# Layer 1's second mixer product: six of eight pairs of token tiles by Strassen's algorithm

## The chip, the cores and the metric

The kernel runs on one core of one Trainium2 chip. The time is device microseconds of one execution, from its launch to its end; 2512.71 us is the median of three runs (2511.84 to 2514.52). The profile is one further execution, read by engine: PE is TensorE (matmuls), PEld its weight loads, DVE is VectorE, ACT is ScalarE, POOL is GpSimd, SP is the engine that issues most DMAs.

## The reference

Two layers, each an attention block and a token mixer, with a residual around each. Only the mixer of the second layer (layer 1) is touched.

```python
x = x + _A_ref(_layernorm(x), ...)          # layer 0: attention
x = x + _B_ref(_layernorm(x), ...)          # layer 0: mixer
x = x + _A_ref(_layernorm(x), ...)          # layer 1: attention
x = x + _B_ref(_layernorm(x), ...)          # layer 1: mixer

def _B_ref(x, w1, b1, w2, b2):              # x: 1 x 2048 tokens x 512 channels
    h = _layernorm(x, axis=-1)
    u = jnp.einsum("bsd,sf->bdf", h, w1) + b1      # contract over the tokens, F = 1792
    u = _gelu(u)
    y = jnp.einsum("bdf,fs->bds", u, w2) + b2      # the second product: contract over F
    return y.transpose(0, 2, 1)
```

The second product gives 2048 tokens x 512 channels and contracts 1792 values of f: `y[s, d] = sum over f of w2[f, s] * u[f, d]`.

## The kernel before

**Numbers in two parts.** Every float32 matrix is split into a first part (rounded to the type `float32r` that TensorE takes) and a second part (the rest). A product is the sum of three matmuls: first by first, first by second, second by first (`split_terms`). ScalarE makes the first part by a copy with a cast, VectorE the second by a subtraction.

**The second product** (`load2`, `split2`, `second`). The tokens are 16 tiles of 128, f is 14 tiles of 128. `u[0]` to `u[13]` hold gelu's result in two parts, 128 values of f by 512 channels each; they stay in SBUF. For token tile s, a block of w2 (1792 x 128) is fetched in two halves of 7 f-tiles (448 KB each), split into two parts, and multiplied: 14 f-tiles x 3 terms = 42 matmuls of 512 columns, all into one PSUM bank. The w2 part is the weight that stays in the array, `u` streams. VectorE then adds bank, bias and `x[s]` in one instruction (L1464), and SP stores `x[s]` to the output (L1608).

**What sets the order.** The order is that in which the program is written. Each engine takes its instructions in order; a wait for another engine holds whatever stands behind it. Halves of w2 are split two or three halves ahead into three buffers (`w2`, 128 x 2 x 7 x 128); a buffer comes free when the matmuls of the half that used it are done, so the ScalarE copy of half k+3 starts when half k's matmuls end. The raw halves have two buffers, and a half is fetched as soon as VectorE has made its second part.

**Before it** (`Mixer.rest`). The last part of the first product leaves `uacc[f]` in SBUF; as each is done, ScalarE takes gelu of it in place (L1424) and casts it to `u[f]` (L1425), VectorE subtracts (L1429). The last tile is f = 13.

**The end.** After the last matmul: L1464 for tile 15, then the store of 256 KB.

Of the kernel before, what the change touches and what calls it, by code (L numbers as in the profile page):

```python
# [8 lines left out]
F32 = mybir.dt.float32  # L9
F32R = mybir.dt.float32r  # L10
# [3 lines left out]
ALU = mybir.AluOpType  # L14
# [4 lines left out]
P = 128  # L19
S, D, H, DH, F = 2048, 512, 32, 16, 1792  # L20
# [3 lines left out]
NKT = S // P  # L24
ND = D // P
NF = F // P
NFH = NF // 2
# [3 lines left out]
HALF = P // 2  # L31
LAG = 2
KEPT = 6
GOING = 8

START = 2
# [14 lines left out]
TINY = (2, 0, 2, -4)  # L51
PLAIN = (2, -2)
FIRST = (1, 2)
NP = 8
NMORE = 4
NQ = 2
# [16 lines left out]
def kernel(  # L73
# [41 lines left out]
    b2c = cp.tile([P, NKT], F32, tag="b2c", name="b2c")  # L115
# [15 lines left out]
    def f32(ap):  # L131
        return ap.bitcast(F32)
# [114 lines left out]
    def split_terms(ah, al, bh, bl_):  # L247
        return ((ah, bh), (ah, bl_), (al, bh))


    class Proj:
# [542 lines left out]
    class Attention:  # L794
# [283 lines left out]
    class Mixer:  # L1078
        def __init__(self, layer):
# [5 lines left out]

            plain, shifted = list(range(NF)), [*range(GOING, NF), *range(GOING)]
            inner = [
# [12 lines left out]
        def open(self):  # L1100
            n = self.l
            self.opened = True
            self.ap = pool(f"uacc{n}")
            self.wp = pool(f"w1p{n}")
            self.hp = pool(f"hp{n}")
            self.uacc = [self.ap.tile([P, D], F32, tag=f"ua{f}", name=f"ua{n}_{f}") for f in range(NF)]

        def norm(self, ts_):

# [119 lines left out]
        def turn(self, att):  # L1229
# [50 lines left out]
        def rest(self, att):  # L1280

            n = self.l
# [37 lines left out]
            b = NB - 1  # L1320
# [43 lines left out]
            att.pp.release()  # L1364
            self.open_u()
            warm(AF.Gelu_apprx_tanh)
            self.load2(0)
            self.load2(1)
            for k, pu in enumerate(going):
                self.product(pu, start=False, stop=False)  # L1370
                self.following()
                if k in (5, 7):
                    self.split2((k - 5) // 2)
            late, begun, turns = [], [], iter(range(2 * NF))

            def finish(f, pu):
# [16 lines left out]
            for together in going[:1], going[1:3], going[3:4], going[4:6], going[6:]:  # L1393
                done = []
# [20 lines left out]

        def open_u(self):
            n = self.l
            self.up = pool(f"up{n}", side="right")
            self.w2p = pool(f"w2p{n}", side="right")
            self.u = [self.up.tile([P, 2, D], F32R, tag=f"u{f}", name=f"u{n}_{f}") for f in range(NF)]  # L1420
# [6 lines left out]
        def gelu_rest(self, f):  # L1427
            tmp = self.uacc[f]
            nc.vector.tensor_tensor(self.u[f][:, 1, :], tmp, f32(self.u[f][:, 0, :]), op=ALU.subtract)  # L1429


        def load2(self, k):
# [36 lines left out]
            self.split2(2 * s + 4)  # L1469

        def close(self):
            self.w2p.release()
            self.up.release()

# [110 lines left out]
    for layer in range(2):  # L1585
        mix = Mixer(layer)
        att.run(mix, proj)
        mix.rest(att)
        more = layer == 0
        if more:  # L1590
            warm(AF.Exp)
            proj = Proj(layer + 1)
        for s in range(NKT):
            b = s // 4 - 1
# [54 lines left out]
        if more:  # L1649
            b = NB - 1  # L1650
# [76 lines left out]
```

## Time and profile before

| what | value |
|---|---|
| median of 3 runs | 2512.71 us |
| span of the profiled execution | 2509.2 us |
| TensorE busy | 2492.8 us, 99% |
| VectorE / ScalarE busy | 62% / 84% |
| layer 1's second product on TensorE | 152.53 us, 672 matmuls |

The profiled execution's span runs from its first to its last instruction; no time of its own is given beside it. The median of the runs is 3.5 us above the span, which is launch and end.

A busy share is read together with the order of work: TensorE is busy nearly always, so what is saved there counts only if nothing else comes to be late. A duration of a matmul (389 ns) holds its way through the array; matmuls follow each other faster than that, so their rate is read from the time of many divided by their count.

### The profile page before, as it was taken

To read this page: it belongs to the slowest core of one execution; us is meant where nothing else is said; L and a number is where in the kernel's file an instruction comes from. 1 tells how busy PE (TensorE), PEld (TensorE's weight loads), DVE (VectorE), ACT (ScalarE), POOL (GpSimd) and SP (SyncE) were. 2 spreads that over 40 slices of the span, in tenths; PEclk is the share of its full clock that TensorE was granted. 3 is DMA by queue.
4 is the path that set the end of the run, shared out by engine and by line. 5 is a ranking of instruction groups with operands and counts; after the bars stand their busy time and mean duration, and the time that the engine had idled before them with its cause. 6 is when DMAs were issued, how large, how long until landed. Compare 5 with 4: busy or idle time off the path is not lost. (4 is left out here: it accounts for less than half of the span.)

```text
span 2509.2 us, 41946 instructions
## 1 busy us (share of the span) xinstructions
PE 2492.8 (99%) x16158; PEld 1240.5 (49%) x16158; DVE 1550.9 (62%) x2458; ACT 2101.7 (84%) x2344; POOL 148.2 (6%) x235
## 2 busy tenths in 40 slices
PE   8999999999999999999999999999999999999999
PEld 6444344444444444588863443444444444445887
DVE  6566566667766776564445664666677667765522
ACT  6999999999999999653349999999999999995511
POOL 5000000000000000141000000000000000002200
PEclk9999999999999999999999999999999999999999
DMA  3221201111111111144423211111111111102343
GB/s 117 75 66 41 65 28 40 31 42 31 39 31 39 31 40 32 41 112 149 126 61 118 58 48 48 31 39 33 39 31 39 32 43 33 40 26 67 106 125 96
DMA packets 168679, 143.56 MB, mean 57 GB/s; under 512 B 17650, under 2 KB 132368, under 8 KB 167952
## 3 DMA queue, kind: packets, MB, share of 16 engines
q1 hardware_dynamic: 168464, 140.72, 19.0%
q8 instruction: 132, 2.16, 0.4%
q14 instruction: 83, 0.68, 0.1%
HBM read 97.67 MB, written 26.22 MB: 49 GB/s over the span
## 5 line engine op out<-in xcount | busy, mean ns | idle before, releaser
L922 ACT ACTIVATE p<-sc 128x1024 f32<-128x1024 f32 x1444 | 1405.8, 1049 | 62.9 <-PE sc L912 62.2
L920 DVE COPY p<-sc 128x1024 f32<-128x1024 f32 x604 | 739.1, 1224 | 522.3 <-PE sc L912 436.4
L928 PE MATMUL acc<-p,vaug 128*32 128x512 f32 x8192 | 1000.1, 599 | 0.5 <-DVE q L531 0.5
L912 PE MATMUL sc<-qs,kst 51*128 51x512 f32 x4096 | 683.5, 432 | 6.8 <-SPq L630 2.7
L922 ACT ACTIVATE p<-p 128x1024 f32<-128x1024 f32 x604 | 655.9, 1086 | 14.1 <-DVE p L920 9.2
L912 PEld LDWEIGHTS sc<-qs,kst 51*128 51x128 f32 x4096 | 338.3, 184 | 559.5 <-ACT p L922 387.3
L928 PEld LDWEIGHTS acc<-p,vaug 128*32 128x32 f32 x8192 | 219.0, 109 | 489.3 <-issue 472.9
L1458 PE MATMUL py<-u,w 128*128 128x512 f32 x1344 | 307.4, 390 | 0.0
L1458 PEld LDWEIGHTS py<-u,w 128*128 128x128 f32 x1344 | 251.9, 188 | 52.3
L1446 ACT CAST w<-w2r 128x896 fp32r<-128x896 f32 x64 | 60.3, 945 | 184.6 <-PE py L1458 177.3
L1205 PE MATMUL pu<-hb,w 128*128 128x512 f32 x792 | 209.6, 406 | 0.0
L1205 PEld LDWEIGHTS pu<-hb,w 128*128 128x128 f32 x792 | 140.9, 188 | 57.7 <-issue 31.9
L1192 POOL TENSOR_TENSOR w<-w1r,w 128x256 fp32r<-128x256 f32 x86 | 70.0, 822 | 1581.5 <-ACT w L1190 1581.1
L1447 DVE TENSOR_TENSOR w<-w2r,w 128x896 fp32r<-128x896 f32 x64 | 72.0, 1124 | 111.4 <-ACT w L1446 111.2
L848 DVE RECIPROCAL o<-o 128x128 f32<-128x128 f32 x120 | 113.3, 944 | 9.4 <-DMA o<-ev 9.4
L889 PE MATMUL po<-wo,hl 128*128 128x512 f32 x360 | 100.4, 412 | 0.1
L830 DVE COPY ev<-acc 128x512 f32<-128x512 f32 x64 | 43.7, 682 | 62.1 <-PE acc L928 62.1
L418 PE MATMUL pq<-hT,wq 128*128 128x512 f32 x312 | 81.1, 404 | 0.0
L889 PEld LDWEIGHTS po<-wo,hl 128*128 128x128 f32 x360 | 62.6, 188 | 33.9 <-issue 16.0
L1205 PE MATMUL pu_l<-hb,w 128*128 128x512 f32 x336 | 77.1, 389 | 0.0
L1464 DVE SCALAR_TENSOR_TENSOR x<-py,b2c,x 128x512 f32<-128x512 f32 x32 | 24.0, 750 | 81.2 <-PE py L1458 81.2
L1190 ACT CAST w<-w1r 128x256 fp32r<-128x256 f32 x86 | 34.5, 406 | 47.1 <-PE pu_l L1205 14.3
(191 smaller groups left out, 1179.0 us busy)
## 6 DMA issues: line engine op xcount, KB each, us to landing
w1r<-in_B_w_dram SPq DMA_DIRECT2D x224, 128.0 KB
w2r<-in_B_w_dram SPq DMA_DIRECT2D x64, 448.0 KB
qs<-qd SPq DMA_DIRECT2D x384, 64.0 KB
qd<-q SPq DMA_DIRECT2D x64, 256.0 KB
o<-ev SPq DMA_DIRECT2D x128, 128.0 KB
x<-in_A_x_dram SPq DMA_DIRECT2D x16, 256.0 KB
hd<-hT SPq DMA_DIRECT2D x2, 2048.0 KB
out_dram<-x SPq DMA_DIRECT2D x16, 256.0 KB
```

The source lines that it names most:

```text
L418: yield nc.tensor.matmul(out, a, c, start=(k == 0), stop=(k == len(terms) - 1))
L848: nc.vector.reciprocal(o[:, 1, c], o[:, 1, c])
L889: nc.tensor.matmul(po, a, c, start=(k == 0), stop=(k == 3 * len(parts) - 1))
L912: nc.tensor.matmul(sc[:, j, :], kst[kt // 4][rows, kt % 4 * P : (kt % 4 + 1) * P], qs[i % NQ][rows, j0 // 2, :], start=True, stop=True,)
L920: nc.vector.tensor_copy(pt, sc)
L922: nc.scalar.activation(pt, sc, AF.Exp, scale=0.25)
L928: nc.tensor.matmul(self.acc[i][c : c + 32, :], vaug[:, kt].rearrange("p d k -> p (d k)"), pt[:, j, :], start=(kt == 0), stop=(kt == NKT - ...
L1192: eng.tensor_tensor(w[:, 1], raw, f32(w[:, 0]), op=ALU.subtract)
L1205: nc.tensor.matmul(pu, a, c, start=(start and k == 0), stop=(stop and k == 5))
L1446: nc.scalar.copy(w[:, 0], raw)
L1447: nc.vector.tensor_tensor(w[:, 1], raw, f32(w[:, 0]), op=ALU.subtract)
L1458: nc.tensor.matmul(py, a, d, start=(c == 0 and f == 0 and k == 0), stop=(c == 1 and f == NFH - 1 and k == 2),)
```

## The change

Two token tiles and the two halves of f make a 2 x 2 matrix of blocks of w2: for tokens 2q and 2q+1 and f-tiles of even and odd number, `A11` (even f, tile 2q), `A12` (odd f, tile 2q), `A21`, `A22` (tile 2q+1). The 512 channels of `u` are cut in two halves of 256: `B11`, `B12` (even f), `B21`, `B22` (odd f). Before, a pair takes the four A blocks, each by 512 columns. By Strassen's algorithm in Winograd's form seven products of a block by 256 columns do it, with sums of A blocks (`S1` to `S4`, made for each pair from w2) and of B blocks (`T1` to `T4`, made once from `uacc`).

Pairs 0 and 1 are multiplied as before, whole (`WHOLE_PAIR`, four products of 21 matmuls of 512 columns; only the f-tiles are now even and odd instead of first and last seven). During their eight products the T sums are made (`inner_sums`: per f-pair k four subtractions of 128 x 256 on VectorE, three casts on ScalarE, three subtractions on VectorE). Pair 2 runs `ENTRY_PAIR`, pairs 3 to 7 `PAIR`: seven products of 21 matmuls of 256 columns. `outer_sum` makes the four S blocks of the next pair on VectorE (128 x 896 each), in place in the raw tiles but for `S1`. Each product's result is added to `x` from PSUM by VectorE, 256 columns at a time. `split_pair(n + 2)` splits two products ahead, into three buffers as before. `load_pair(q + 2)` fetches four raw blocks (448 KB each). All of it is for layer 1; layer 0 keeps its code.

```diff
+ENTRY_PAIR = (
+    ("A11", "B11", "X", True, ("11b",)), ("A12", "B21", "Z", True, ("11",)),
+    ("S2", "T2", "X", False, ("12b",)), ("S4", "B22", "Y", True, ("12",)),
+    ("S3", "T3", "X", False, ("22b",)), ("S1", "T1", "Y", True, ("12", "22")),
+    ("A22", "T4", "X", False, ("21b",)),
+)
+PAIR = (
+    ("A11", "B11", "X", True, ("11b",)), ("A12", "B21", "Z", True, ("11",)),
+    ("S2", "T2", "X", False, ("12b",)), ("S1", "T1", "Y", True, ("22b",)),
+    ("S3", "T3", "X", False, ("22",)), ("S4", "B22", "Y", False, ("12",)),
+    ("A22", "T4", "X", False, ("21b",)),
+)
+NPAIR, NWHOLE = NKT // 2, 2
+PAIRS = [WHOLE_PAIR] * NWHOLE + [ENTRY_PAIR] + [PAIR] * (NPAIR - NWHOLE - 1)
...
             warm(AF.Gelu_apprx_tanh)
-            self.load2(0)
-            self.load2(1)
+            if n:
+                self.load_pair(0, RAWS[:2])
...
                 self.gelu_rest(g)
+            if n:
+                self.begin_pairs()
+                return
...
+        def inner_sums(self, k):
...
+            sub(t1, b[:, 0, 1], b[:, 0, 0])
+            sub(tmp[:, 1], b[:, 1, 1], b[:, 0, 1])
+            sub(tmp[:, 0], b[:, 1, 1], t1)
+            sub(tmp[:, 2], b[:, 1, 0], tmp[:, 0])
...
+            for i, out in enumerate(outs):
+                nc.scalar.copy(out[:, 0], tmp[:, i])
+            for i, out in enumerate(outs):
+                nc.vector.tensor_tensor(out[:, 1], tmp[:, i], f32(out[:, 0]), op=ALU.subtract)
...
+        def split_pair(self, n):
...
+            p, bufs = (self.w2q, 2) if n % 3 else (self.w2p, 1)
+            w = self.w2[n] = p.tile([P, 2, NFH, P], F32R, tag="w2", bufs=bufs, name=f"w2_{n}")
+            self.split(w, self.raw[self.lefts[n]])
...
+        def pairs(self):
...
+                for j, entry in enumerate(table):
+                    self.split_pair(n + 2)
+                    self.beside(q, j, n)
+                    self.block(q, n, banks[entry[2]], *entry)
+                    n += 1
+
+        def beside(self, q, j, n):
+            if q < NWHOLE:
+                if n < NFH:
+                    self.inner_sums(n)
+                if j == 2:
+                    self.load_pair(q + 2)
+                if q == NWHOLE - 1:
+                    if j == 1:
+                        self.outer_sum(q + 1, "S1")
+                    self.outer_sum(q + 1, ("S1", "S3", "S2", "S4")[j]) if j else None
+                return
+            if q == NWHOLE and j < 4:
+                for k in range(2 * j, min(2 * j + 2, NFH)):
+                    self.split(self.operand("T1", k), self.t1[k])
+            if j > 2:
+                self.outer_sum(q + 1, ("S1", "S3", "S2", "S4")[j - 3])
+            if j == 5:
+                self.load_pair(q + 2)
+
+        def block(self, q, n, py, left, right, key, start, outs):
...
+                    terms, out = split_terms(w[:, 0, k], w[:, 1, k], t[:, 0], t[:, 1]), py[:, :HD]
+                for i, (a, c) in enumerate(terms):
+                    nc.tensor.matmul(
+                        out, a, c, start=start and k == i == 0, stop=(k == NFH - 1 and i == 2),
+                        skip_group_check=True,
+                    )
...
+        if not more:
+            mix.pairs()
+            mix.close()
+            break
```

How the instructions stand, at three places. First VectorE before, at output tiles 2 to 4 of layer 1 (`w_1_k` is the split w2 half k, `x_70` is token tile 2):

```order
L1464 SCALAR_TENSOR_TENSOR x_70<-py_2_24519,b2c,x_70 128x512
L1447 TENSOR_TENSOR w_1_8_24568<-w2r_8_24516,w_1_8_24568 128x896
L1447 TENSOR_TENSOR w_1_9_24596<-w2r_9_24544,w_1_9_24596 128x896
L1464 SCALAR_TENSOR_TENSOR x_71<-py_3_24574,b2c,x_71 128x512
L1447 TENSOR_TENSOR w_1_10_24623<-w2r_10_24571,w_1_10_24623 128x896
L1447 TENSOR_TENSOR w_1_11_24651<-w2r_11_24599,w_1_11_24651 128x896
L1464 SCALAR_TENSOR_TENSOR x_72<-py_4_24629,b2c,x_72 128x512
```

Per tile there are two subtractions for w2 and one addition to `x`. Now VectorE from the end of the two whole pairs into pair 2 (`w_n` is the split block n, `tt`, `t_6` and `qs_90` the last T sums, `rA` and `rS` the raw blocks and S sums of pair 2, `u_k<-t_j` the second part of T1, `x_72` token tile 4, `py` the banks X and Z, `pyy` the bank Y):

```order
L1485 TENSOR_TENSOR t_6_24652<-tt_24647,t_6_24652 128x256 x2
L1485 TENSOR_TENSOR qs_90<-tt_24647,qs_90 128x256
L1512 TENSOR_TENSOR rA_2_24494<-rS_2_24617,rA_2_24494 128x896
L1466 TENSOR_TENSOR w_9_24689<-rA_2_24496,w_9_24689 128x896
L1512 TENSOR_TENSOR rA_2_24496<-rA_2_24496,rA_2_24494 128x896
L1588 SCALAR_TENSOR_TENSOR x_71<-pyy_24563,b2c,x_71 128x512
L1466 TENSOR_TENSOR w_10_24718<-rA_2_24494,w_10_24718 128x896
L1466 TENSOR_TENSOR u_0_24010<-t_0_24405,u_0_24010 128x256
L1466 TENSOR_TENSOR u_2_24012<-t_1_24442,u_2_24012 128x256
L1588 SCALAR_TENSOR_TENSOR x_72<-py_24716,b2c,x_72 128x256
L1466 TENSOR_TENSOR w_11_24747<-rA_2_24496,w_11_24747 128x896
L1466 TENSOR_TENSOR u_4_24014<-t_2_24481,u_4_24014 128x256
```

Between two subtractions for w2 there stood at most one addition; now the T sums, an S sum or two parts of T1 stand there, and the first addition of pair 2 (`x_72`) stands behind all of them. Second, VectorE in a pair further on (pair 4's blocks from the second on, and the S sums for pair 5):

```order
L1588 SCALAR_TENSOR_TENSOR x_76<-py_25115,b2c,x_76 128x256
L1466 TENSOR_TENSOR w_25_25142<-rS_4_25003,w_25_25142 128x896
L1592 TENSOR_TENSOR x_76<-x_76,py_25115 128x256
L1466 TENSOR_TENSOR w_26_25167<-rA_4_24868,w_26_25167 128x896
L1588 SCALAR_TENSOR_TENSOR x_76<-py_25115,b2c,x_76 128x256
L1466 TENSOR_TENSOR w_27_25192<-rA_4_24866,w_27_25192 128x896
L1507 TENSOR_TENSOR rS_5_25195<-rA_5_25061,rA_5_25063 128x896
L1588 SCALAR_TENSOR_TENSOR x_77<-pyy_25116,b2c,x_77 128x256
L1466 TENSOR_TENSOR w_28_25219<-rA_4_24870,w_28_25219 128x896
L1512 TENSOR_TENSOR rA_5_25061<-rA_5_25057,rA_5_25061 128x896
L1592 TENSOR_TENSOR x_77<-x_77,py_25115 128x256
```

Each block has a subtraction for w2 and an addition of 256 columns, four of seven blocks have an S sum as well. Third, TensorE before, from output tile 11 to 12:

```order
L1458 MATMUL py_11_25014<-u_11_24035,w_1_23_24981 128x512 x3
L1458 MATMUL py_11_25014<-u_12_24036,w_1_23_24981 128x512 x3
L1458 MATMUL py_11_25014<-u_13_24037,w_1_23_24981 128x512 x3
L1458 MATMUL py_12_25069<-u_0_24024,w_1_24_25008 128x512 x3
L1458 MATMUL py_12_25069<-u_1_24025,w_1_24_25008 128x512 x3
```

and now, from block 44 (A12 by B21, f-tiles of odd number) to block 45 (S2 by T2, which `t_k` holds):

```order
L1579 MATMUL py_25683<-u_11_24021,w_44_25656 128x256 x3
L1579 MATMUL py_25683<-u_13_24023,w_44_25656 128x256 x3
L1579 MATMUL py_25683<-t_0_24411,w_45_25685 128x256 x3
L1579 MATMUL py_25683<-t_1_24448,w_45_25685 128x256 x3
L1579 MATMUL py_25683<-t_2_24487,w_45_25685 128x256 x3
```

A row was three matmuls of 512 columns and is three of 256; the number of blocks in a pair goes from four to seven.

## Rows read from the trace of the kernel before

**Rows 1.** The page: busy time, share and count of each engine.

```profile
span 2509.2 us, 41946 instructions
PE 2492.8 (99%) x16158; PEld 1240.5 (49%) x16158; DVE 1550.9 (62%) x2458; ACT 2101.7 (84%) x2344; POOL 148.2 (6%) x235
```

**Rows 2.** Chain of waits, its last pieces: start us, us, what.

```profile
2479.83 25.40 PE py L1458 x112
2505.23 0.02 issue
2505.25 0.75 DVE x L1464
```

**Rows 3.** Windows, layer 1's second product: us, busy by engine (x), granted clock, DMA.

```profile
core 0: us, PE busy (x) PEld busy (x) DVE busy (x) ACT busy (x) POOL busy (x), PEclk, DMA share, GB/s
2352.69:2505.22 152.53, 152.53 (x673) 125.98 (x671) 46.60 (x49) 30.56 (x34) 0.00 (x0) 1.00 0.38 111
```

**Rows 4.** Timeline, one output tile: start us, us, engine line op xcount [idle before].

```profile
2381.49 0.95 ACT L1446 CAST w<-w2r 128x896 fp32r<-128x896 f32 x1 [3.81 <-PE py L1458]
2381.49 0.75 DVE L1464 SCALAR_TENSOR_TENSOR x<-py,b2c,x 128x512 f32<-128x512 f32 x1 [2.69 <-PE py L1458]
2382.47 1.09 DVE L1447 TENSOR_TENSOR w<-w2r,w 128x896 fp32r<-128x896 f32 x1 [0.23 <-ACT w L1446]
```

**Rows 5.** Timeline, TensorE: matmuls in a row, four kinds.

```profile
2352.69 152.53 PE L1458 MATMUL py<-u,w 128*128 128x512 f32 x672
...
149.25 1.04 PE L552 MATMUL pc<-sq,sel 128*32 128x512 bf16 x4
...
14.73 2.84 PE L137 MATMUL pk<-ident 128*128 128x128 f32 x24
```

**Rows 6.** Lines, TensorE: mean ns of one, for the three kinds.

```profile
L1458 PE MATMUL py<-u,w 128*128 128x512 f32 x1344 | 307.4, 390 | 0.0
L552 PE MATMUL pc<-sq,sel 128*32 128x512 bf16 x31 | 8.3, 382 | 0.0
L137 PE MATMUL pk<-ident 128*128 128x128 f32 x24 | 2.8, 275 | 0.0
```

**Rows 7.** Timeline, weight loads: two in a row; those of the product.

```profile
37.42 0.30 PEld L418 LDWEIGHTS pk<-hT,wkv 128*128 128x128 f32 x2
...
2352.46 152.33 PEld L1458 LDWEIGHTS py<-u,w 128*128 128x128 f32 x672
```

**Rows 8.** By line, L1458: duration of one, minimum, median, maximum.

```profile
L1458 PEld LDWEIGHTS py<-u,w x1344: 187/188/192, 1107.2 to 2504.6; 128*128 128x128 f32 x192
```

**Rows 9.** Timeline, VectorE and ScalarE where the second product begins.

```profile
2352.89 0.69 DVE L1213 TENSOR_TENSOR ua<-ua,pu_l 128x512 f32<-128x512 f32 x1 [0.68 <-PE pu_l L1205]
2353.49 1.29 DVE L1429 TENSOR_TENSOR u<-ua,u 128x512 fp32r<-128x512 f32 x2
2355.02 0.69 DVE L1429 TENSOR_TENSOR u<-ua,u 128x512 fp32r<-128x512 f32 x1 [0.24 <-ACT u L1425]
...
2354.89 0.94 ACT L1446 CAST w<-w2r 128x896 fp32r<-128x896 f32 x1
```

**Rows 10.** Lines, VectorE and ScalarE: operations of the sizes that the change adds.

```profile
L1192 DVE TENSOR_TENSOR w<-w1r,w 128x256 fp32r<-128x256 f32 x138 | 58.7, 425 | 4.8
L897 DVE TENSOR_TENSOR x<-x,po 128x512 f32<-128x512 f32 x64 | 43.9, 686 | 26.7 <-PE po L889 26.7
L1190 ACT CAST w<-w1r 128x256 fp32r<-128x256 f32 x86 | 34.5, 406 | 47.1 <-PE pu_l L1205 14.3 <-PE pu_b L1205 7.4 <-DMA w1r<-in_B_w_dram 6.8
```

**Rows 11.** Windows, while w2 is fetched (columns as in rows 3).

```profile
2376.00:2377.50 1.50, 1.50 (x9) 1.23 (x8) 0.00 (x0) 0.77 (x1) 0.00 (x0) 1.00 1.00 315
2377.50:2379.00 1.50, 1.50 (x8) 1.26 (x7) 1.09 (x1) 0.18 (x1) 0.00 (x0) 1.00 0.26 98
```

**Rows 12.** Timeline, after the last matmul.

```profile
2505.25 0.75 DVE L1464 SCALAR_TENSOR_TENSOR x<-py,b2c,x 128x512 f32<-128x512 f32 x1 [8.77 <-PE py L1458]
2506.03 0.33 SPq L1608 DMA_DIRECT2D out_dram<-x  x1
```

More of the change, by code (lines that the diff above doesn't have):

```diff
@@ L33 @@
 KEPT = 6
+HD = D // 2
 GOING = 8
@@ L53 @@
 FIRST = (1, 2)
+RAWS = ("A11", "A12", "A21", "A22")
+WHOLE_PAIR = tuple((name, None, "XXYY"[i], i % 2 == 0, (str(i // 2 + 1),) * (i % 2)) for i, name in enumerate(RAWS))
+ENTRY_PAIR = (
[4 rows of a table added]
+)
+PAIR = (
[4 rows of a table added]
+)
+NPAIR, NWHOLE = NKT // 2, 2
+PAIRS = [WHOLE_PAIR] * NWHOLE + [ENTRY_PAIR] + [PAIR] * (NPAIR - NWHOLE - 1)
 NP = 8
@@ L1105, in open @@
             self.hp = pool(f"hp{n}")
-            self.uacc = [self.ap.tile([P, D], F32, tag=f"ua{f}", name=f"ua{n}_{f}") for f in range(NF)]
+            both = [self.ap.tile([P, 2, D], F32, tag=f"ua{k}", name=f"ua{n}_{k}") for k in range(NFH)]
+            self.both = both
+            self.uacc = [both[f // 2][:, f % 2, :] for f in range(NF)]
         def norm(self, ts_):
@@ L1366, in rest @@
             warm(AF.Gelu_apprx_tanh)
-            self.load2(0)
-            self.load2(1)
+            if n:
+                self.load_pair(0, RAWS[:2])
+            else:
+                self.load2(0)
+                self.load2(1)
             for k, pu in enumerate(going):
@@ L1371, in rest @@
                 self.following()
-                if k in (5, 7):
+                if not n and k in (5, 7):
                     self.split2((k - 5) // 2)
+                elif k == 7:
+                    self.split_pair(0)
+                    self.load_pair(0, RAWS[2:])
             late, begun, turns = [], [], iter(range(2 * NF))
@@ L1417, in open_u @@
             n = self.l
+            self.raw, self.t23, self.t1 = {}, {}, {}
+            self.t4 = [k.rearrange("p (k c) -> p k c", k=2) for k in kst]
+            self.t4 += [qs[0][:, j].rearrange("p (k c) -> p k c", k=2) for j in range(2)]
+            self.t4 += [qs[1][:, 0].rearrange("p (k c) -> p k c", k=2)]
+            self.lefts = [(q, entry[0]) for q, table in enumerate(PAIRS) for entry in table]
             self.up = pool(f"up{n}", side="right")
@@ L1429, in gelu_rest, with split @@
             nc.vector.tensor_tensor(self.u[f][:, 1, :], tmp, f32(self.u[f][:, 0, :]), op=ALU.subtract)
+        def split(self, out, src):
+            nc.scalar.copy(out[:, 0], src)
+            nc.vector.tensor_tensor(out[:, 1], src, f32(out[:, 0]), op=ALU.subtract)
+        def inner_sums(self, k):
+            n = self.l
+            b = self.both[k].rearrange("p f (j c) -> p f j c", j=2)
+            t1 = self.t1[k] = self.w2q.tile([P, HD], F32, tag=f"t1_{k}", name=f"t1_{k}")
+            tmp = self.pair_pool(k).tile([P, 3, HD], F32, tag="tt", name=f"tt_{k}")
+            sub = lambda out, u, v: nc.vector.tensor_tensor(out, u, v, op=ALU.subtract)
+            sub(t1, b[:, 0, 1], b[:, 0, 0])
+            sub(tmp[:, 1], b[:, 1, 1], b[:, 0, 1])
+            sub(tmp[:, 0], b[:, 1, 1], t1)
+            sub(tmp[:, 2], b[:, 1, 0], tmp[:, 0])
+            t23 = self.ap.tile([P, 2, 2, HD], F32R, tag=f"ua{k}", name=f"t{n}_{k}")
+            self.t23[k] = t23
+            outs = t23[:, 0], t23[:, 1], self.t4[k]
+            for i, out in enumerate(outs):
+                nc.scalar.copy(out[:, 0], tmp[:, i])
+            for i, out in enumerate(outs):
+                nc.vector.tensor_tensor(out[:, 1], tmp[:, i], f32(out[:, 0]), op=ALU.subtract)
@@ new lines, in pair_pool, with load_pair @@
+        def pair_pool(self, q):
+            return self.w2q if q % 2 else self.w2p
+        def load_pair(self, q, names=RAWS):
+            if q >= NPAIR:
+                return
+            for name in names:
+                j = RAWS.index(name)
+                s, c = 2 * q + j // 2, j % 2
+                src = w2_d[:, s * P : (s + 1) * P].rearrange("(t c p) s -> c p t s", p=P, c=2)[c]
+                raw = self.pair_pool(q).tile([P, NFH, P], F32, tag=f"r{name}", name=f"r{name}_{q}")
+                nc.sync.dma_start(raw, src)
+                self.raw[q, name] = raw
@@ new lines, in outer_sum @@
+        def outer_sum(self, q, name):
+            if not NWHOLE <= q < NPAIR:
+                return
+            raw = self.raw
+            if name == "S1":
+                s1 = raw[q, "S1"] = self.w2p.tile([P, NFH, P], F32, tag="rS1", name=f"rS1_{q}")
+                nc.vector.tensor_tensor(s1, raw[q, "A21"], raw[q, "A22"], op=ALU.add)
+                return
+            a, b, out = {
+                "S3": ("A11", "A21", "A21"), "S2": ("S1", "A11", "A11"), "S4": ("A12", "S2", "A12")
+            }[name]
+            nc.vector.tensor_tensor(raw[q, out], raw[q, a], raw[q, b], op=ALU.subtract)
+            raw[q, name] = raw[q, out]
@@ new lines, in split_pair, with begin_pairs @@
+        def split_pair(self, n):
+            if n >= len(self.lefts):
+                return
+            p, bufs = (self.w2q, 2) if n % 3 else (self.w2p, 1)
+            w = self.w2[n] = p.tile([P, 2, NFH, P], F32R, tag="w2", bufs=bufs, name=f"w2_{n}")
+            self.split(w, self.raw[self.lefts[n]])
+        def begin_pairs(self):
+            self.hp.release()
+            self.wp.release()
+            self.w2q = pool("w2q")
+            self.split_pair(1)
+            self.load_pair(1)
@@ new lines, in operand @@
+        def operand(self, name, k):
+            if name[0] == "B":
+                c = int(name[2]) - 1
+                return self.u[2 * k + int(name[1]) - 1][:, :, c * HD : (c + 1) * HD]
+            if name == "T1":
+                return self.u[2 * k][:, :, HD:]
+            return self.t4[k] if name == "T4" else self.t23[k][:, int(name[1]) - 2]
+        def pairs(self):
+            n = 0
+            for q, table in enumerate(PAIRS):
+                both = bank2(f"py_{q}")
+                banks = {"X": both[:, 0], "Z": both[:, 1], "Y": bank(q, f"pyy_{q}")}
+                for j, entry in enumerate(table):
[3 more added lines that the diff above has]
+                    n += 1
@@ new lines, in block @@
+        def block(self, q, n, py, left, right, key, start, outs):
+            w = self.w2.pop(n)
+            for k in range(NFH):
+                if right is None:
+                    u = self.u[2 * k + int(left[2]) - 1]
+                    terms, out = split_terms(w[:, 0, k], w[:, 1, k], u[:, 0], u[:, 1]), py
+                else:
+                    t = self.operand(right, k)
+                    terms, out = split_terms(w[:, 0, k], w[:, 1, k], t[:, 0], t[:, 1]), py[:, :HD]
[4 more added lines that the diff above has]
+                    )
+            done = set()
+            for to in outs:
+                s = 2 * q + int(to[0]) - 1
+                c = slice((int(to[1]) - 1) * HD, int(to[1]) * HD) if len(to) > 1 else slice(0, D)
+                if len(to) != 2:
+                    nc.vector.scalar_tensor_tensor(
+                        x[s][:, c], out, b2c[:, s : s + 1], x[s][:, c], op0=ALU.add, op1=ALU.add
+                    )
+                else:
+                    nc.vector.tensor_tensor(x[s][:, c], x[s][:, c], out, op=ALU.add)
+                if len(to) == 1:
+                    done.add(s)
+            if right and left in ("A22", "S4" if PAIRS[q] is PAIR else "S1"):
+                done.add(2 * q + (left == "A22"))
+            for s in done:
+                nc.sync.dma_start(xout[:, s, :], x[s])
@@ L1471, in close @@
         def close(self):
+            if self.l:
+                self.w2q.release()
+                self.ap.release()
             self.w2p.release()
```

1 line of the change is left out of this document (added).

## Prediction

> **What bounds the kernel now.** I read the page first: TensorE is busy 2492.8 of 2509.2 us, the next engine ScalarE 84%, VectorE 62% [rows 1]. The reader is to see that a saving on TensorE counts nearly in full, but only where the others keep up in that very stage. The chain of waits ends in the second product's matmuls, 0.75 us of VectorE behind them and the store [rows 2]. So I opened that stage by windows: 152.53 us, TensorE busy in all of it at granted clock 1.00 (the 2.4 GHz level), VectorE 46.6 us, ScalarE 30.6 us, GpSimd nothing [rows 3]. In one tile's timeline both waited for TensorE 2.7 and 3.8 us before they took up work at once when a block ended [rows 4]. TensorE alone bounds the stage, and VectorE has about 106 us to give there. GpSimd's absence from the new code changes nothing: it does nothing here already.
>
> **Removed: matmul columns.** The 672 matmuls span 152.53 us, the last one 0.39 long: (152.53 - 0.39) / 671 = 226.7 ns each [rows 5, 6]. A whole pair has 84 of them: 19.04 us. A Strassen pair has 7 x 21 = 147 matmuls of 256 columns. At exactly half the rate that is 147 x 113.3 = 16.66 us, but no row shows a float32r matmul of 256 columns, so its pitch is bounded from both sides.
>
> - Low end. Plain float32 matmuls of 128 columns, each with a new 128-column weight, come every (2.84 - 0.275) / 23 = 111.5 ns [rows 5, 6]. Two float32r weight loads in a row take 0.30 us, one 0.188, so the second starts 0.11 us after the first [rows 7, 8]. A new weight for each matmul costs about 111 ns however short the matmul is. I don't go below it.
> - High end with hidden loads. At 2.4 GHz 512 columns take 213.3 ns; were the other 13.4 ns paid once per matmul, 256 columns would take 120 ns.
> - Between them: four bf16 matmuls of 512 columns with a narrow weight took (1.04 - 0.382) / 3 = 219 to 220 ns [rows 5, 6]. So some 7 of 226.7 ns don't belong to the columns. Half of 220, and 7 kept: 117 ns. This I take.
> - The far end: a load that doesn't hide at all, 188 ns and a few to start the matmul, 191 ns [rows 8]. The product speaks against it: 672 loads lie over the same 152 us as 672 matmuls [rows 5, 7], which 188 + 213 = 401 ns each would not allow. But today a load has 227 ns of cover, and would have 117.
>
> With 117 ns a pair takes 17.20 us, 1.84 less; six pairs give 11.0 us (15.9 at 111.5; 8.4 at 120). Pairs 0 and 1 keep their 84 matmuls of 512.
>
> **Added: VectorE work beside the whole pairs.** The cost is nothing only as long as TensorE covers it, so I worked its queue through in order. Operations without a wait between them overlap a little: two of 0.69 us took 1.29 [rows 9], so the second started 0.60 us after the first and each costs 0.08 to 0.09 less than its duration. A subtraction of 128 x 256 is 0.425 us [rows 10], so 0.34 in a row; one of 128 x 896 is 1.09 [rows 4], 1.01 in a row. One T set: four subtractions, the last two dependent, 1.57; a 0.41 us cast on ScalarE before the first of the remaining three can start, 0.44; three of 0.34; together about 3.05. With the block's w2 subtraction that is 4.1 us, and 0.67 for an addition of 512 columns every other block: 4.4 of the 4.76 us that a block of 21 wide matmuls takes. VectorE starts late, though. It still has gelu's rest until 2355.7 [rows 9], then the w2 subtraction of block 1 until 2356.95 (needed at 2357.45), and ends each T set some 3.5 us after the block that it stands beside. That lag stays, and beside blocks 5 to 7 the four S sums add 4.2 us. It ends the whole pairs about 4.0 us behind TensorE.
>
> Then blocks take 2.46 us, and VectorE has the w2 subtraction and two T1 parts (1.01 + 0.68) ahead of the addition of block 8. That addition reads bank X, and block 10 writes X again: TensorE gets there at 2390.77 + 4.9 = 2395.7, VectorE is through at about 2396.9, and TensorE waits 1.4 us with the release. Block 9 gets its weights just in time. By the end of pair 2 the lag is down to 1.9 us and holds nothing.
>
> **Later pairs.** Seven w2 subtractions (7.1), four S sums (4.4), seven additions of 256 columns: 128 x 512 from PSUM is 0.686 [rows 10] or 0.75 [rows 4], 256 columns fewer save 0.26, so 0.41 to 0.35 in a row, 2.7 in all. That is 14.2 us of 17.2. In the four blocks with an S sum VectorE falls up to 1.3 us behind; a bank is written again one block (2.46 us) after its block has ended, so nothing waits. ScalarE's seven casts (6.7 us) fit easily. SP: a pair fetches 4 x 448 KB and stores 2 x 256 KB, 2.36 MB in 17.2 us, 137 GB/s; one fetch ran at 315 GB/s [rows 11], so four blocks need 5.8 us. They are issued beside the sixth block and first used five blocks (12.3 us) later. The store queued behind them is late by their issue only.
>
> **Moved: the beginning.** With f-tiles taken even first, u[12] is needed 18 matmuls (4.1 us) into the product instead of 36. It is ready at 2353.49 + 1.29 = 2354.8 [rows 9], needed at 2356.8: no cost. If that cover went, each us late would be one us of TensorE.
>
> **The end.** The last addition has 256 columns instead of 512: 0.75 [rows 12] less 0.26. The store behind it is the same 256 KB.
>
> Sum on the profiled span: -11.0 + 1.4 - 0.3 = -9.9, 2499.3 us. The runs' median lies 3.5 us above the span, so 2502.8 us.
>
> **Rivals.**
> A. VectorE's operations don't overlap, or a step of the T sets takes longer. At full duration and a handoff of 0.03 us each, the queue is 5.1 us per whole block instead of 4.4, VectorE comes 11 us late to pair 2, and TensorE waits in blocks 8 to 14 for weights and banks, 9 to 10 us together: 2511 to 2513. For it: seven new operations per block on the one engine with a queue to make up. Against it: the 1.29 us row. The Trainium skill (VectorE: DVE Perf Modes, "The DRAIN you can't avoid") says that the next operation doesn't start until the pipeline of the last is empty. By this rule A would hold; the trace doesn't agree, with 0.60 us from start to start of operations of 0.69 us. Chance 0.14.
>
> B. The slower side: the weight load of 128 columns becomes the bound of a 256-column matmul. At 191 ns a pair takes 28.1 us, 9.0 more, six pairs +54 us: about 2567. It decides from 129.5 ns on, where 147 narrow matmuls equal 84 wide ones. Against it stands the 0.11 us between two loads; for it, that no row has float32r loads at that pace for long. The Trainium skill (TensorE: Matmul & The Clock Gate, Part 3, "The mechanism") states that a weight load overlaps matmuls in flight only when its row group differs. Here all loads fill all 128 rows, so B would hold by that rule; the trace of before disagrees, at 226.7 ns for a 188 ns load and 512 columns. Chance 0.08.
>
> C. The fetch of w2 comes late for the S sums, by perhaps 2 us per pair: 2514 to 2515. At 315 GB/s it has 6 us in hand; chance 0.03.
>
> **Numbers.** My forecast holds with chance 0.75 and has its own range of 2498 (111.5 ns and 1.6 us of wait) to 2505.5 (120 ns). The range for 8 in 10 takes in most of A: 2497.5 to 2511. A measurement of this kernel tells 0.2%, 5.0 us, from no change. Faster by more: the forecast nearly whole and a part of A, 0.77. Within: most of A, C, and a pitch near 128 ns, 0.11. Slower: B and mishaps of A's kind that are worse, 0.12.
>
> **What would show it.** The pitch of the narrow matmuls: (time of a block) / 21; 111 to 120 ns is right, 130 or more wrong. One gap on TensorE of 1 to 2 us where S2 by T2 of pair 2 begins, ended by VectorE's addition of the block two before; several there would be A. VectorE busy over 80% from pair 3 on, without a gap on TensorE. Six pairs of 17 to 18 us each. The forecast is wrong if TensorE waits in later pairs too, or if weight loads, not VectorE, end its waits.

## The result: slower by 0.28%, and the profile after

The changed kernel took 2519.50 us (median of 7 executions, 2514.75 to 2519.88) beside 2511.84 us for the kernel before (7 executions, 2509.47 to 2514.52): a ratio of 1.0028, with an interval of 1.0017 to 1.0039. Forecast were 2502.8 us and a range that ended at 2511.0. The profiled execution is the shortest of the seven: 2514.75 us, span 2513.0, which is 3.8 us more than before, where the sum had said 9.9 less.

The page of the changed kernel, the lines that answer to [rows 1]:

```profile
span 2513.0 us, 42927 instructions
PE 2488.0 (99%) x16536; PEld 1252.8 (50%) x16536; DVE 1623.0 (65%) x2587; ACT 2127.2 (85%) x2390; POOL 147.5 (6%) x235
```

TensorE is busy 4.8 us less than before, and yet the end comes 3.8 us later. So there are some 8.6 us more in which it stands still. Its share is 99% as before: a share of the whole span doesn't show them. The windows do, here the two whole pairs, pair 2, and two of the five later pairs, which take 19.29 to 19.32 us each (columns as in [rows 3]):

```profile
2352.68:2391.61 38.93, 38.93 (x170) 31.53 (x168) 33.67 (x68) 16.98 (x34) 0.00 (x0) 1.00 0.46 123
2391.61:2412.60 20.99, 18.01 (x148) 17.65 (x147) 18.00 (x28) 8.73 (x14) 0.00 (x0) 1.00 0.58 161
2412.60:2431.90 19.30, 18.02 (x150) 17.66 (x149) 14.83 (x20) 6.60 (x7) 0.00 (x0) 1.00 0.43 124
...
2489.81:2509.13 19.32, 18.05 (x149) 17.65 (x147) 9.40 (x13) 4.70 (x5) 0.00 (x0) 1.00 0.09 34
```

A pair of 84 wide matmuls took 19.04 us before. Each Strassen pair is longer than that, and TensorE is idle in 1.3 us of a later pair and in 3.0 us of pair 2. (A block's row is 2.68 us long, but the next block starts 2.52 us after it where nothing waits; before a wait the row's end doesn't overlap the next, so the idle time understates what the pair loses.) The timeline of TensorE from pair 2's first block to pair 3's third shows where (start us, us, what, and in brackets the idle time before it with what ended it):

```profile
2391.61 2.68 PE L1579 MATMUL py<-u,w 128*128 128x256 f32 x21
2396.66 2.75 PE L1579 MATMUL py<-u,w 128*128 128x256 f32 x21 [2.37 <-DVE x L1588]
2400.02 2.74 PE L1579 MATMUL py<-t,w 128*128 128x256 f32 x21 [0.61 <-DVE x L1592]
2402.59 2.68 PE L1579 MATMUL pyy<-u,w 128*128 128x256 f32 x21
2405.11 2.63 PE L1579 MATMUL py<-t,w 128*128 128x256 f32 x21
2407.57 2.68 PE L1579 MATMUL pyy<-u,w 128*128 128x256 f32 x21
...
2412.60 2.68 PE L1579 MATMUL py<-u,w 128*128 128x256 f32 x21
2415.95 2.75 PE L1579 MATMUL py<-u,w 128*128 128x256 f32 x21 [0.67 <-DVE x L1588]
2419.31 2.75 PE L1579 MATMUL py<-t,w 128*128 128x256 f32 x21 [0.61 <-DVE x L1592]
```

A block that waits for nothing and follows one that didn't starts 2.46 to 2.52 us after the one before; that is 117 to 120 ns per narrow matmul, which no row before showed [rows 5]. But block 9 (the second row) starts 5.05 us after block 8, block 10 3.36 us after block 9, and the first two steps of pair 3 are 3.35 and 3.36 us. All waits are for VectorE's additions to `x`, and they come twice in each of the six pairs. The view of waits, TensorE alone, over the product (total us, times, longest):

```profile
PE py L1579 <- DVE x L1588: 5.7, 6, 2.4
PE py L1579 <- DVE x L1592: 3.6, 6, 0.6
```

Here L1588 is the addition of block 0 of a pair (bank X), L1592 that of block 1 (bank Z). The idle times sum to 9.3 us; against the pitch of 2.52 us the blocks start later by a bit more, 0.83 and 0.84 us where the view says 0.67 and 0.61, because a row ends 2.68 us after its start (2.75 behind a wait), later than the start of a next block that doesn't wait (2.52).

VectorE in pair 2's beginning, from the subtraction for block 10's weights on:

```profile
2394.37 1.08 DVE L1466 TENSOR_TENSOR w<-rA,w 128x896 fp32r<-128x896 f32 x1
2395.37 0.75 DVE L1466 TENSOR_TENSOR u<-t,u 128x256 fp32r<-128x256 f32 x2
2396.04 0.48 DVE L1588 SCALAR_TENSOR_TENSOR x<-py,b2c,x 128x256 f32<-128x256 f32 x1
...
2399.45 0.42 DVE L1592 TENSOR_TENSOR x<-x,py 128x256 f32<-128x256 f32 x1 [1.26 <-PE py L1579]
```

The addition of block 8 ends at 2396.52 and block 9 starts at 2396.66: it is this operation that lets it go. From then on VectorE itself waits for TensorE (1.26 us ahead of the next addition), so it is no longer behind; and yet block 10 waits for that addition too.

The end answers to [rows 12]: an addition of 0.48 us instead of 0.75, and the store as before.

```profile
2509.33 0.48 DVE L1588 SCALAR_TENSOR_TENSOR x<-py,b2c,x 128x256 f32<-128x256 f32 x1 [2.08 <-PE py L1579]
2509.85 0.33 SPq L1598 DMA_DIRECT2D out_dram<-x  x1
```

### The profile page after: what moved, and what is told of

Read it like the earlier page. It is cut to its first block, busy times and chain, and to the rows that moved or that the text cites. A ratio compares the mean times of both kernels' runs of the same rounds, so it can differ in the third digit from the quotient of the medians.

```text
span 2513.0 us, 42927 instructions
## 1 busy us (share of the span) xinstructions
PE 2488.0 (99%) x16536; PEld 1252.8 (50%) x16536; DVE 1623.0 (65%) x2587; ACT 2127.2 (85%) x2390; POOL 147.5 (6%) x235
## 5 line engine op out<-in xcount | busy, mean ns | idle before, releaser
L1627 PE MATMUL py<-u,w 128*128 128x512 f32 x672 | 154.8, 390 | 0.0
L1627 PEld LDWEIGHTS py<-u,w 128*128 128x128 f32 x672 | 125.7, 188 | 26.1
L1615 ACT CAST w<-w2r 128x896 fp32r<-128x896 f32 x32 | 30.0, 943 | 76.8 <-PE py L1627 69.5
L1465 ACT CAST w<-rA 128x896 fp32r<-128x896 f32 x44 | 41.3, 942 | 62.3 <-PE py L1579 44.4
L1616 DVE TENSOR_TENSOR w<-w2r,w 128x896 fp32r<-128x896 f32 x32 | 37.1, 1159 | 52.2 <-ACT w L1615 52.2
```

The lines of the kernel that those rows point to most:

```text
L1627: nc.tensor.matmul(py, a, d, start=(c == 0 and f == 0 and k == 0), stop=(c == 1 and f == NFH - 1 and k == 2),)
```

## The experiments

The theory after this reading: banks X and Z are the two halves of one tile (`both`). The release of a tile goes by the whole tile, so block 1's first matmul, which writes only Z, waits until VectorE has read X. The rival: VectorE's queue is late, whichever bank it reads. The comparisons of again, banks, banks_pool and all_whole share one set of runs of the kernel before (27 executions, median 2510.75, 2508.07 to 2514.87); that of place has its own.

**again: the changed kernel once more.** No edit.

> The changed kernel as it is, for a second profile and the spread of its times. Its first profiled execution spans 2513.0 us, 3.8 above the kernel before, while most of its executions take 4.7 us more than that one, at a mean granted clock of 0.997 instead of 0.998. Theory (clock): TensorE's waits in pair 2 (2.4 and 0.6 us) and the two in each later pair make the granted clock fall for a stretch in most executions; a profile of a slow one shows half clock between 2391 and 2509 us, and its Strassen pairs are longer than 19.3 us. Rival (place unrelated): the half clock lies in the attention or at the beginning, and the Strassen pairs take 19.3 us as before; then the 4.7 us have nothing to do with the second product.

Measured: 2516.17 us (11 executions, 2513.47 to 2520.02), ratio 1.0020 (1.0011 to 1.0029). The slowdown stands, somewhat smaller than first measured; the profile has the same waits. The profiled execution (2513.47 us) has no half clock in the product and Strassen pairs of 19.3 us, so it doesn't decide between the theory of the clock and its rival; look_b and look_c do.

**banks: X and Z in tiles of their own.**

```diff
-                both = bank2(f"py_{q}")
-                banks = {"X": both[:, 0], "Z": both[:, 1], "Y": bank(q, f"pyy_{q}")}
+                banks = {"X": bank2(f"py_{q}")[:, 0], "Y": bank(q, f"pyy_{q}")}
+                if q >= NWHOLE:
+                    banks["Z"] = bank(q + 1, f"pyz_{q}")
```

> Bank Z is a tile of its own (the other single bank) and no longer the second half of X's two-bank tile; nothing else. Theory (shared tile): the matmuls of a pair's second block wait for VectorE's addition of the first block, which reads the other half of the same tile, and those of the third for the addition of the second. Two starts of 0.85 us too late in each pair go: pairs 3 to 7 take 147 x 0.120 = 17.6 us instead of 19.3, pair 2 about 19 instead of 21.0, the span 2513.0 - 5 x 1.7 - 2 = 2502 to 2503.5. Rival (VectorE late): the additions are late by themselves, and the waits come back one block further on, for bank X or for a w2 block: pairs stay at 19 us or more, the span above 2510.

Measured: 2503.51 us (7 executions, 2500.54 to 2507.00), ratio 0.9969 (0.9958 to 0.9981). Nothing else differs from the changed kernel: the same operations in the same order on each engine. Windows of banks, the whole pairs, pair 2 and two later pairs:

```profile
2355.96:2394.89 38.93, 38.93 (x169) 31.53 (x168) 33.67 (x68) 16.98 (x34) 0.00 (x0) 1.00 0.47 123
2394.89:2412.98 18.09, 17.77 (x149) 17.59 (x147) 17.75 (x28) 8.74 (x14) 0.00 (x0) 1.00 0.67 186
2412.98:2430.51 17.53, 17.53 (x149) 17.53 (x148) 14.82 (x20) 6.61 (x7) 0.00 (x0) 1.00 0.47 136
...
2483.16:2500.75 17.59, 17.59 (x149) 17.54 (x147) 9.42 (x13) 4.71 (x5) 0.00 (x0) 1.00 0.10 38
```

A later pair takes 17.53 to 17.59 us without a gap, 1.75 less than in the changed kernel, with VectorE just as busy (14.8 us). That decides against the rival. The view of waits, TensorE, has one row left:

```profile
PE pyz L1580 <- DVE x L1589: 0.3, 1, 0.3
```

It stands ahead of block 9: the bank that Z takes at the entry is the one in which token tile 3 lay, and its addition comes late. Here VectorE's lag does count, 0.5 to 0.6 us of it.

**banks_pool: as banks, with pair 2's four S sums on GpSimd.**

```diff
+            eng = nc.gpsimd if q == NWHOLE else nc.vector
...
-                nc.vector.tensor_tensor(s1, raw[q, "A21"], raw[q, "A22"], op=ALU.add)
+                eng.tensor_tensor(s1, raw[q, "A21"], raw[q, "A22"], op=ALU.add)
...
-            nc.vector.tensor_tensor(raw[q, out], raw[q, a], raw[q, b], op=ALU.subtract)
+            eng.tensor_tensor(raw[q, out], raw[q, a], raw[q, b], op=ALU.subtract)
```

> As the run with Z in its own bank, and the four S sums of pair 2 are made by GpSimd instead of VectorE. Theory (queue at the entry): what is left of TensorE's wait in pair 2 comes from VectorE's queue, which the four S sums (1.08 us each) make longer; without them pair 2 takes 17.6 to 18.0 us, and the span is 1 to 2 us below the run with separate banks alone. Rival: GpSimd takes about 2.9 us for a sum (0.82 for 128x256), 11.5 in a row, so S4 comes after the point where block 11 wants it, or it slows VectorE's own operations beside it: the span is no shorter, or longer.

Measured: 2505.84 us (9 executions, 2504.71 to 2509.92), ratio 0.9977 (0.9967 to 0.9987). The intervals of banks and banks_pool overlap, but nothing was won: the timeline, VectorE and GpSimd beside the second whole pair, then with TensorE about pair 2's beginning:

```profile
2379.56 2.26 POOL L1508 TENSOR_TENSOR rS<-rA,rA 128x896 f32<-128x896 f32 x1 [27.34 <-DMA rA<-in_B_w_dram]
2379.75 2.35 DVE L1474 TENSOR_TENSOR t<-ua 128x256 f32<-128x256 f32 x1
2381.90 2.19 POOL L1513 TENSOR_TENSOR rA<-rA,rA 128x896 f32<-128x896 f32 x1
2382.03 2.35 DVE L1474 TENSOR_TENSOR tt<-ua 128x256 f32<-128x256 f32 x1
...
2393.04 2.85 POOL L1513 TENSOR_TENSOR rA<-rS,rA 128x896 f32<-128x896 f32 x1 [8.95 <-DVE w L1466]
2393.47 0.42 DVE L1474 TENSOR_TENSOR tt<-ua,t 128x256 f32<-128x256 f32 x1
2393.93 2.23 DVE L1474 TENSOR_TENSOR tt<-ua,tt 128x256 f32<-128x256 f32 x1
...
2399.32 2.10 POOL L1513 TENSOR_TENSOR rA<-rA,rA 128x896 f32<-128x896 f32 x1 [3.44 <-issue]
2399.76 2.60 DVE L1466 TENSOR_TENSOR w<-rA,w 128x896 fp32r<-128x896 f32 x1
2399.99 4.19 PE L1581 MATMUL pyz<-u,w 128*128 128x256 f32 x21 [2.20 <-DVE x L1590]
```

Beside each of GpSimd's four sums one VectorE subtraction was held: three that take 0.42 us elsewhere took 2.35, 2.35 and 2.23, one of 1.09 took 2.60, and they ended 0.3 us (the last 0.9) after the GpSimd operation beside them. The Trainium skill (SBUF — State Buffer, "Who interferes with whom") states that an instruction with two SBUF inputs on VectorE and a GpSimd instruction that reads SBUF exclude each other for a whole instruction. The four long rows agree with it; the row of 0.42 us, which lies within the third GpSimd span, doesn't, though spans on GpSimd are rough. So 4.3 us of sums (four of 1.08) left VectorE and 7.2 us of longer subtractions came in their place, as the rival had it, and TensorE waited 2.2 us where banks waited 0.3. The block behind that wait shows something else: 4.19 us for 21 matmuls instead of 2.7. The window of that stretch (columns as in [rows 3], the granted clock is the third number from the end):

```profile
2399.90:2403.30 3.40, 3.31 (x15) 3.34 (x16) 3.40 (x4) 1.56 (x3) 1.52 (x1) 0.51 0.45 138
```

0.51 is the lower level, 1.2 GHz, for 3.4 us behind a wait of 2.2 us.

**all_whole: all eight pairs whole.** The T and S sums are left out; the product is computed as before the change, but in the new code's order and buffers.

```diff
-NPAIR, NWHOLE = NKT // 2, 2
-PAIRS = [WHOLE_PAIR] * NWHOLE + [ENTRY_PAIR] + [PAIR] * (NPAIR - NWHOLE - 1)
+NPAIR, NWHOLE = NKT // 2, 8
+PAIRS = [WHOLE_PAIR] * NWHOLE
...
-                if n < NFH:
-                    self.inner_sums(n)
```

> All eight pairs whole, no T or S sums: the changed order of f-tiles, raw blocks and buffers without Strassen's algorithm. Theory (buffer place): in the changed kernel's whole pairs the blocks whose split w2 lies in the newly opened pool come at 233.3 ns per matmul, the others at 227.9; it is the place of the buffer, so here 21 or 22 of 32 blocks are slow, the product takes 152.5 + 21 x 21 x 0.0055 = 155 us, the span 2511.5 to 2512. Rival (VectorE's work): the T sums beside these blocks slow TensorE's reads; without them all blocks come at 227 ns and the span is 2509.

Measured: 2514.48 us (11 executions, 2511.58 to 2518.09), ratio 1.0016 (1.0007 to 1.0025). The 0.85 us that the two whole pairs lose (38.93 instead of 2 x 19.04 us) aren't VectorE's T sums: without them the same pairs take the same time. Windows of all_whole, TensorE only (us, busy with its count, granted clock, DMA share, GB/s), the first two pairs and the other six:

```profile
2356.05:2394.98 38.93, 38.93 (x170) 1.00 0.58 152
2394.98:2511.82 116.84, 116.84 (x505) 1.00 0.33 91
```

The other six take 116.84, 19.47 each; the product is 155.8 us long, 3.2 more than before [rows 3]. TensorE's blocks follow each other 4.90 us apart (233.3 ns per matmul) or 4.80 to 4.82 us apart (228.6 to 229.4), and the faster ones are blocks 0, 3, 6 and so on: those whose split weights lie in the older pool (`w2p`, one buffer). The others lie in the new pool (`w2q`, two buffers).

**entry: as banks, Z of pair 2 from another tile.**

```diff
-                    banks["Z"] = bank(q + 1, f"pyz_{q}")
+                    z = f"pyz_{q}"
+                    banks["Z"] = bank2(z)[:, 0] if q == NWHOLE else bank(q + 1, z)
```

> As banks, but bank Z of the entry pair alone is taken from a two-bank tile whose first user (the first whole pair) has long been read. Theory (the last wait, 0.6 us before block 9, is for the addition of token tile 3, which stood in the bank that Z takes): no wait of TensorE longer than 0.1 us from the first whole pair to the end; pair 2 takes 17.6 us as the later ones, 0.6 us less than in banks. Block 10 then starts at the entry some 0.5 us after the addition of block 8 has ended, so it still holds nothing. Rival (VectorE's lag, whichever bank): the wait moves to block 10, 0.5 us or more, ended by the addition of block 8, and the pair is as long as in banks. Time about 0.6 us less than banks, less than a measurement tells.

Measured: one execution of 2503.48 us, span 2501.8. No wait of TensorE in the product is left, and pair 2 takes 17.65 us:

```profile
2392.47:2410.12 17.65, 17.65 (x148) 17.61 (x147) 17.58 (x28) 8.75 (x14) 0.00 (x0) 1.00 0.68 192
```

VectorE's addition of block 8 and TensorE's block 10, from the timelines:

```profile
2396.90 0.48 DVE L1590 SCALAR_TENSOR_TENSOR x<-py,b2c,x 128x256 f32<-128x256 f32 x1
2397.53 2.75 PE L1581 MATMUL py<-t,w 128*128 128x256 f32 x21
```

So at the entry VectorE's lag holds next to nothing once each bank is released by itself. But the margin of 0.5 us that was expected isn't there: the addition ends at 2397.38 and block 10 starts 0.15 us later, which is the hand-over alone (in the changed kernel 2396.52 to 2396.66). Block 10 comes 2.55 us after block 9 instead of 2.52.

**place: as entry, two split buffers in the older pool, one in the new.**

```diff
-            p, bufs = (self.w2q, 2) if n % 3 else (self.w2p, 1)
+            p, bufs = (self.w2p, 2) if n % 3 < 2 else (self.w2q, 1)
...
-            tmp = self.pair_pool(k).tile([P, 3, HD], F32, tag="tt", name=f"tt_{k}")
+            tmp = self.w2q.tile([P, 3, HD], F32, tag="tt", bufs=2, name=f"tt_{k}")
...
-                s1 = raw[q, "S1"] = self.w2p.tile([P, NFH, P], F32, tag="rS1", name=f"rS1_{q}")
+                s1 = raw[q, "S1"] = self.w2q.tile([P, NFH, P], F32, tag="rS1", name=f"rS1_{q}")
```

> As entry, and two of the three buffers of split blocks lie in the older pool, one in the newer (before: one and two); the first S sum and the temporaries of the T sums go to the newer pool instead. Theory (the 5 ns per wide matmul hang on which pool the weights' buffer lies in): wide blocks 0, 1, 3, 4, 6 and 7 run at 228 to 229 ns per matmul and blocks 2 and 5 at 233; in banks it is 0, 3 and 6 that run at 228. The whole pairs together get some 0.3 us shorter. Rival (the number of the block, or which of three buffers it is, counts): blocks 0, 3 and 6 stay alone at 228. Narrow blocks stay at 119 to 120 ns everywhere. Time against the kernel before: 0.996 to 0.997, some 1 us less than banks.

Measured: 2502.85 us (5 executions, 2501.47 to 2506.60) beside 2511.87 (9 executions, 2510.38 to 2515.01), ratio 0.9966 (0.9952 to 0.9979). The windows of blocks 1, 2 and 3 (TensorE only, columns as in all_whole's), and of the whole pairs and pair 2 (columns as in [rows 3]):

```profile
2356.78:2361.55 4.77, 4.77 (x23) 1.00 0.44 110
2361.55:2366.45 4.90, 4.90 (x23) 1.00 0.02 9
2366.45:2371.24 4.79, 4.79 (x22) 1.00 0.92 241
...
2351.97:2390.48 38.51, 38.51 (x169) 31.53 (x168) 33.25 (x67) 16.98 (x34) 0.00 (x0) 1.00 0.45 120
2390.48:2408.55 18.07, 17.79 (x148) 17.61 (x147) 18.00 (x28) 8.74 (x14) 0.00 (x0) 1.00 0.69 193
```

Block 1 in the changed kernel (columns as in [rows 3]):

```profile
2357.50:2362.40 4.90, 4.90 (x23) 3.94 (x22) 4.03 (x10) 1.87 (x4) 0.00 (x0) 1.00 0.02 5
```

And TensorE's timeline in place, blocks 9 and 10:

```profile
2393.00 2.68 PE L1581 MATMUL pyz<-u,w 128*128 128x256 f32 x21
2395.96 2.74 PE L1581 MATMUL py<-t,w 128*128 128x256 f32 x21 [0.28 <-DVE x L1590]
```

Block 1, at 233 ns before, now takes 4.77 us / 21 = 227 ns, block 2, still in the new pool, 233, block 3 228. So the rate goes with the pool in which the buffer lies, and not with the block's number. What about the place costs the 5 ns (the address, what lies beside it; the temporaries changed pools too) wasn't tried. The pairs won 0.42 us, and with that TensorE came to block 10 before VectorE did: block 10 starts 2.96 us after block 9, 0.44 late, behind the addition of block 8. This is the very wait that the prediction had put at 1.4 us. Place and banks can't be told apart by their times; both beat the kernel before.

**look_b and look_c: the changed kernel, two more profiles.** No edit; the question is why most of its executions are some 5 us longer than the one profiled first.

> The changed kernel as it is, for one more profile. Its executions lie between 2513 and 2520 us, at a mean granted clock of 0.999 down to 0.996, and both profiles so far are of its short ones. Theory of the long ones (the wait of 2.4 us at the entry to pair 2 lets the clock fall to its lower level for the block behind it, as a wait of 2.2 us did in banks_pool): an execution of 2516 us or more shows a stretch of half clock within pair 2, block 9 at about 195 ns per matmul. Rival (the clock falls elsewhere, as in the kernel before): the stretches of half clock of a long execution lie outside the product, at the beginnings of the attention stages, and pair 2 takes 21.0 us as in the first profile. In a short execution neither is told apart.

> The same kernel and the same question as look_b, for a second profile: half clock behind the entry's wait (pair 2 longer than 22 us) or elsewhere only (pair 2 at 21.0 us). The waits of 1.7 us in each of the pairs 3 to 7 are the same in any execution.

Measured: 2519.95 and 2519.59 us, spans 2518.2 and 2517.9, both long ones. Windows of look_b, TensorE only (third number: granted clock): the stretch behind the wait at the entry, pair 2, and the beginning of layer 1's attention; last, from the first profile of the changed kernel, block 9 up to block 10:

```profile
2400.50:2403.90 3.40, 3.40 (x17) 0.50 0.74 200
2395.36:2417.87 22.51, 19.52 (x148) 0.92 0.55 154
1301.40:1308.20 6.80, 6.38 (x27) 0.50 0.74 212
...
2396.66:2400.02 3.36, 2.75 (x22) 1.00 0.73 196
```

In both, TensorE stood still for 2.38 us ahead of block 9 and then ran at half clock, which lasted 3.4 us: pair 2 takes 22.51 us in look_b and 22.33 in look_c instead of 20.99. In the first profile and in again the same wait has no half clock behind it. The half clock at the beginning of the attention stages is in the kernel before as well, for 3.4 us at a time in its profile, and 6.8 here and in banks. Of the 5.2 us between the spans of look_b and the first profile, 1.5 are pair 2, and 3.7 had been lost before the product began (2356.43 instead of 2352.68). Theory and rival were both right, for 1.5 and 3.7 us. Why the same wait is followed by half clock in one execution and not in another stays open.

## Why the prediction was wrong, point by point

**What bounds the kernel: right.** TensorE bounds the stage; wherever it doesn't wait, the end moves by its columns.

**The pitch of the narrow matmuls: right in its bounds, mis-sized by 2.5 ns.** I took 117 ns; banks shows 17.55 us / 147 = 119.4. The high end of 120, by which the 13 ns beside the columns are paid once per matmul, was nearly it; the bf16 row, from which I took 7 ns, was not the nearer one. Six pairs give 6 x (19.04 - 17.55) = 8.9 us instead of 11.0.

**Rival B falls.** Weight loads take 186 to 193 ns and hide beneath matmuls 117 to 120 ns apart. The Trainium skill's sentence (TensorE: Matmul & The Clock Gate, Part 3, "The mechanism") that a load overlaps matmuls in flight only in another row group is contradicted by this trace once more, with loads of all 128 rows. The same section also says that a load into the background weight buffer is pulled ahead of matmuls in flight, by which B would not hold; no run here shows that buffer itself.

```profile
L1579 PEld LDWEIGHTS py<-t,w x252: 186/189/193, 2400.0 to 2503.9; 128*128 128x128 f32 x126
```

**VectorE's queue beside the whole pairs: right, and rival A falls.** The first three subtractions of a T set:

```profile
2357.86 0.42 DVE L1474 TENSOR_TENSOR t<-ua 128x256 f32<-128x256 f32 x1
2358.20 0.42 DVE L1474 TENSOR_TENSOR tt<-ua 128x256 f32<-128x256 f32 x1
2358.53 0.42 DVE L1474 TENSOR_TENSOR tt<-ua,t 128x256 f32<-128x256 f32 x1
```

They start 0.34 us apart, and the third, which needs the first's result, 0.33 behind the second, as taken. The Trainium skill's section named for A (VectorE: DVE Perf Modes, "The DRAIN you can't avoid") goes on to say that a next operation that isn't held starts earlier, which I had left out. These rows agree with that part, so the section doesn't speak for A. The addition of block 8 was to be through at 2396.9 and was at 2396.52.

**The step that failed:** "a bank is written again one block (2.46 us) after its block has ended, so nothing waits". It counted banks, and the kernel waits by tiles. X and Z are one tile, and block 1 writes Z right behind block 0, whose sum in X VectorE reads only then. So a tile is written again not one block later but at once, and what was to be hidden by a whole block (a release, 0.48 us of addition and a release back) lies on TensorE's path: 0.83 us ahead of block 1, and ahead of block 2, which writes X, the same for the addition of Z. The spans differ from the forecast by 13.7 us: 8.8 are these waits in pairs 3 to 7, 2.0 the longer wait at the entry, the rest is the pitch (2.1) and the whole pairs (0.85). That this could be seen beforehand is the lesson: in the rows of the order both additions of a pair's first two blocks read one buffer (`py_25115`), and the matmuls of blocks 44 and 45 write one (`py_25683`), while Y has its own.

**The wait at the entry: right in its cause, one block too early and bigger.** It was given as 1.4 us ahead of block 10, for the addition of block 8. Through the shared tile block 9 already waited for it: 2.53 us, and block 10 another 0.84. With banks apart and the whole pairs quicker, in place, it stood where it was predicted, with 0.44 us; in entry, where each bank is released by itself as well but the whole pairs take 0.42 us longer, they had just hidden it.

**Not in the sum: the place of the new buffers.** "Pairs 0 and 1 keep their 84 matmuls of 512" was costed at nothing more; they lose 0.85 us, of which place gave 0.42 back.

The sum on the profiled spans, from predicted to measured terms:

| term | predicted | measured |
|---|---|---|
| narrow matmuls, six pairs | -11.0 | -8.9 |
| entry pair's waits | +1.4 | 20.99 - 17.55 = +3.4 |
| waits in pairs 3 to 7 | 0 | 5 x (19.30 - 17.55) = +8.8 |
| whole pairs | 0 | +0.85 |
| last addition | -0.3 | -0.27 |
| sum | -9.9 | +3.9 (spans: +3.8) |

**The median above the span.** I took 3.5 us between the profiled span and the median for launch and end. The first profiled execution of the changed kernel shows 2514.75 - 2513.0 = 1.75; the rest is clock, which differs from execution to execution. The median lies 6.5 us above that short execution's span; in look_b there are 1.75 us of launch and end, 3.7 lost outside the product, where the kernel before has its half clock too, and 1.5 behind the entry's wait, which that kernel doesn't have. So launch and end take 1.7 to 1.8 us in every execution on record, of the kernel before too, and not 3.5.

**Rival C falls:** no wait in the product is for a DMA. ScalarE, the S sums and the store at the end were as worked out.

Measured against what would have shown the forecast wrong ("if TensorE waits in later pairs too"), the timeline says it at once. With each bank in its own tile the change is worth 0.31% (banks, beside 2510.75 us), where the forecast had 0.39%.

## What to carry to other kernels

Before a wait is costed at nothing because a buffer is written again late, ask by which unit it is released: two banks in one tile are one buffer, and matmuls that alternate between them wait for each read. Where blocks get shorter, a hand-over to another engine and back, here 0.83 us, that was hidden by a block ahead must still have a whole block to hide in. And a wait as long as the one at the entry here (2.4 us) should be priced with the half clock that may follow it: 1.3 to 1.5 us in two of four profiles.

## What the runs showed of the hardware that wasn't expected

- A float32r matmul of 256 columns comes every 117 to 120 ns and one of 512 every 226.7 at best: at 2.4 GHz their columns take 106.7 and 213.3 ns, which leaves 10 to 13 ns for each matmul beside the columns (an estimate from these pitches).
- The rate of 512-column matmuls goes with the pool in SBUF in which their weights lie: 227.1 to 229.4 ns in one pool, 233.2 to 233.4 in the other, in all nine profiles of the new code. With 256 columns the only blocks below 119 ns (117.3 to 118.6) have their weights in the older pool too, and multiply by a T sum; with halves of `u` blocks of that pool come at 119 to 120 too.
- After one and the same wait of 2.4 us the granted clock fell to its lower level for 3.4 us in two executions of the changed kernel and not in two others, and once after one of 2.2 us (banks_pool); behind waits of 0.3 to 0.7 us it never fell in the product.
- Beside each of four GpSimd operations one VectorE operation ended only after it: 0.42 us became 2.23 to 2.35, 1.09 became 2.60.
